# Decode attention over two KV caches: the loads of V issued by GpSimd on a second DMA queue

## The chip, the cores and the metric

The kernel runs on 1 core of one Trainium2 chip. The core has five instruction streams that run side by side and meet only in semaphores: TensorE (PE), VectorE (DVE), ScalarE (ACT), GpSimd (POOL) and SyncE (SP). SP does no arithmetic here; it issues DMAs. The core's 16 DMA engines move the data from HBM (the chip's main memory) to SBUF (the core's working memory) for whichever stream issued the DMA. The metric is the device time of one execution in microseconds, the median of several runs; a smaller number is better.

## The reference

Two independent blocks, A and B, each a one-token decode step of multi-head attention over a cache, with 8 sequences, 32 heads, 4096 cached positions and 128 numbers per head, all in bf16. The outputs are laid side by side.

```
def _A_ref(x, k_cache, v_cache, wq, wo):
    B, Sq, D = x.shape                      # 8, 1, 1024
    H, Dh = 32, 128
    q = transpose((x @ wq).reshape(B, Sq, H, Dh), 0, 2, 1, 3)
    scores = jnp.einsum("bhqd,bhkd->bhqk", q, k_cache) * (Dh ** -0.5)
    p = _softmax(scores, axis=-1)
    o = jnp.einsum("bhqk,bhkd->bhqd", p, v_cache)
    return transpose(o, 0, 2, 1, 3).reshape(B, Sq, H * Dh) @ wo
...
return jnp.concatenate([a, b], axis=-1)     # the same for B
```

Every byte of both K caches and both V caches is read once, and little is done with each: the caches are 4 x 268 MB of the 1107 MB that the kernel moves.

## The kernel before

The work is cut into 64 steps, numbered n: 2 blocks x 4 groups of 8 heads x 8 sequences. One step handles 8 heads of one sequence. Its K is 8 heads x 4096 positions x 128 numbers, 8 MiB, laid out as 128 partitions of 64 KB: each head takes 16 partitions, each partition 256 positions. Its V has the same shape.

In step n the engines do this:

- DVE multiplies K(n) in place by the broadcast query, in four chunks of 64 positions (`multiply`, the costliest DVE line).
- PE adds up each product over the 128 numbers by 16 matmuls against the identity into PSUM (`add_up`), and DVE finishes the sum (`reduce`), chunk by chunk, through two PSUM tiles. DVE then finds the maximum (`softmax`).
- PE multiplies the probabilities of the step before with V(n-1) (`pv`, 64 matmuls).
- ACT takes the eight exponentials (`exps`) into `prob`. There is one `prob`, so `exps(n)` starts only when `pv(n-1)` has read the old one.
- ACT copies the result of `pv` out of PSUM (`copy_o`), PE gathers it (`gather`) and adds up the row sums (`rowsum`), DVE normalises (`heads`, `invert`), and GpSimd copies 128 x 8 numbers to their place (`ona<-on`).

PE runs its stream in order: four `add_up`, then `pv(n-1)`, then in every second step the broadcast of the next two queries (`make_qbc`, from a tile `qg` that GpSimd has filled in `pick_q`), then `gather` and `rowsum`, then the `add_up` of step n+1.

Three buffers hold the caches: `kbuf` has two halves, so K(n) goes to half n % 2, and `vbuf` is one buffer of 8 MiB for V. V(m) can be written only after `pv(m-1)` has read V(m-1). K(n+2) can be written only after the last `add_up(n)` has read the products of K(n). The weights wq, and at the end wo, are loaded through the same buffers.

The order of the work is the order in which the Python code adds operations: a small class, `Program`, keeps a list per engine, derives the waits from the names that each operation reads and writes, drops those that an earlier wait already implies (through `op.clock`), and rolls the steady part into loops. Before the change SP issues all loads of K, V and the weights, in one list: `load_k(n)`, then `load_v(n-1)`, for each n. An issue that has to wait holds the issues behind it. What SP issues goes through one DMA queue, called q1 in the profile; the loads of x and some stores go through ACT's queue, q10.

Of the kernel before, what the change touches and what calls it, by code (L numbers as in the profile page):

```python
# [27 lines left out]
class Program:  # L28
# [33 lines left out]
    def finish(self):  # L62
        for op in self.ops:
            op.deps = [d for d in op.deps if d.dma or d.eng != op.eng or op.eng != "pe"]
            for d in op.deps:
                d.sig = True
        for e in ENGINES:
            ops = self.order[e]
            for a, b, k in self.loops[e]:
                size = (b - a) // k  # L70
                assert size * k == b - a, (e, a, b, k)
                for p in range(a, a + size):
                    if any(ops[p + i * size].sig for i in range(k)):
                        for i in range(k):
                            ops[p + i * size].sig = True
        counts = {}
        for op in self.ops:
            if op.dma:
                counts[op.dma] = counts.get(op.dma, 0) + 16
                op.token = (op.dma, counts[op.dma])  # L80
        for e in ENGINES:
            k = 0
            for op in self.order[e]:
                if op.sig and not op.dma:
                    k += 1
                    op.token = (e, k)
        known = {e: {} for e in ENGINES}
        for op in self.ops:
            mine = known[op.eng]
            waits = {}  # L90
            for d in sorted(op.deps, key=lambda d: -d.token[1]):
                key, val = d.token
                if mine.get(key, 0) >= val:
                    continue
                waits[key] = max(val, waits.get(key, 0))
                for k2, v2 in d.clock.items():
                    if mine.get(k2, 0) < v2:
                        mine[k2] = v2
            op.deps = waits
            op.clock = dict(mine)  # L100
            if op.token:
                op.clock[op.token[0]] = max(op.token[1], op.clock.get(op.token[0], 0))
        return counts
# [40 lines left out]
def _build(nc, caches, out):  # L144
# [23 lines left out]
    with es:  # L168
# [53 lines left out]
        def dma(eng, dst, src, writes, sem, reads=()):  # L222
            return P.add(eng, lambda e: e.dma_start(dst, src), reads=reads, writes=writes, dma=sem)  # L223
# [78 lines left out]
        def source(c, what, b, g):  # L302
            return caches[c][what][b, g * HP:(g + 1) * HP].rearrange("h (p t) d -> (h p) (t d)", t=T)

        def where(n):
            gi, b = divmod(n, B)
            c, g = divmod(gi, NG)
            return c, g, b
# [5 lines left out]
        def load_v(m):  # L314
            c, g, b = where(m)
            buf, name = (vbuf[:], "v") if m < NS - 1 else (kbuf[:, m % 2, :], f"k{m % 2}")
            dma("sp", buf, source(c, 2, b, g), [name], name)
            vplace[m] = (buf, name)

        def load_wo(c):  # L320
# [219 lines left out]
        NS = NC * NG * B  # L540
# [13 lines left out]
        for n in range(NS):  # L554
            m = n - 1
# [9 lines left out]
            if m >= 0:  # L565
                load_v(m)
# [24 lines left out]
            if n == NS - 1:  # L591
                load_v(n)
                project(0, 0)
                write_out(0)
                load_wo(1)
# [128 lines left out]
```

## Time and profile before

| what | value |
|---|---|
| median of 3 runs | 2559.11 us (2558.98 to 2559.45) |
| the profiled execution, its own time | 2558.87 us |
| its span, first to last instruction | 2557.6 us |
| busy: PE, DVE, ACT, POOL | 58%, 53%, 25%, 11% |
| moved by DMA | 1107.49 MB |

The profile shows one execution. A page gives totals, a row of digits for 40 slices of the span, the DMA queues, the chain of work that ended last, and the costliest groups of instructions. A group's row reads: line, engine, operation, output<-inputs, shapes, count | busy us, mean ns of one | idle us of the engine ahead of it and what ended that idle time. The timeline lists instructions by start (us) and duration (us), with the idle time ahead of them in brackets. SPq, ACTq and POOLq are the issuing streams of DMAs.

### The profile page before, as it was taken

The numbers are of one execution on the slowest core, as the hardware profiler recorded it, in microseconds if no ns is written. First come the engines' busy times: TensorE is split into PE (matmuls) and PEld (weight loads), VectorE is DVE, ScalarE is ACT, GpSimd is POOL, SyncE is SP. The second block draws the span as 40 slices with busy tenths as digits, with TensorE's granted clock in tenths as the row PEclk, the third lists the DMA queues.
The fourth block names the chain that finished last, engine by engine and source line by source line (L and its number), as shares of the span: only waits on it lengthen the run. The fifth ranks groups of instructions, "written<-read, shape, count | busy, mean of one in ns | idle before, by whom it ended". The sixth has DMA issues, their size and how long they took to land.

```text
span 2557.6 us, 18705 instructions
## 1 busy us (share of the span) xinstructions
PE 1479.5 (58%) x9322; PEld 286.9 (11%) x5308; DVE 1360.2 (53%) x912; ACT 651.6 (25%) x1129; POOL 291.2 (11%) x112
## 2 busy tenths in 40 slices
PE   3565565565565565565565565565655655655658
PEld 0001101101101101101011011011011011011012
DVE  3455455455465465464565564564564564554551
ACT  0322322312313313313313213223223223223132
POOL 0111011011011011011011011011011110110110
PEclk8787887787887887887877887877877877877879
DMA  9999999999999999999999999999999999999999
GB/s 426 428 439 430 439 430 438 430 439 429 439 430 436 434 433 437 430 438 430 439 430 439 430 439 430 438 432 438 432 436 433 436 432 436 434 433 437 430 439 398
DMA packets 19834, 1107.49 MB, mean 433 GB/s; under 512 B 2240, under 2 KB 2272, under 8 KB 2672
## 3 DMA queue, kind: packets, MB, share of 16 engines
q1 hardware_dynamic: 19744, 1107.31, 99.9%
q8 instruction: 5, 0.08, 0.0%
q10 hardware_dynamic: 80, 0.06, 0.0%
q14 instruction: 5, 0.04, 0.0%
HBM read 1107.33 MB, written 0.03 MB: 433 GB/s over the span
## 4 chain that ended last, share of the span: by engine, by line
DMA 62%; PE 17%; DVE 14%; issue 6%; SPq 1%; another core or an unknown queue 0%; DVEq 0%
DMA kbuf<-in_B_k_cache_dram 31%; DMA kbuf<-in_A_k_cache_dram 30%; PE red L357 12%; DVE kbuf L347 12%; PE oacc L406 4%; DVE osb L369 2%; DMA kbuf<-in_B_wo_dram 1%; SPq L223 0%; PE acc L490 0%; PE late L490 0%; DVE on L433 0%; DVEq L656 0%; PE oacc L255 0%; PE late L255 0%
## 5 line engine op out<-in xcount | busy, mean ns | idle before, releaser
L347 DVE TENSOR_TENSOR kbuf<-kbuf,qbc 128x8192 bf16<-128x8192 bf16 x256 | 1128.3, 4408 | 779.2 <-DMA kbuf<-in_B_k_cache_dram 380.4
L357 PE MATMUL red<-kbuf,ident 128*128 128x512 bf16 x4096 | 1050.0, 418 | 388.4 <-DVE kbuf L347 217.1
L385 ACT ACTIVATE prob<-osb,bias 128x256 bf16<-128x256 f32 x512 | 598.9, 1584 | 904.8 <-PE oacc L406 870.3
L435 POOL COPY ona<-on 128x8 bf16<-128x8 bf16 x64 | 278.7, 4355 | 2211.3 <-DVE on L433 2211.3
L421 PE MATMUL sps<-sel,osb 128*128 128x8 f32 x512 | 116.6, 357 | 650.1 <-ACT osb L413 650.0
L369 DVE TENSOR_REDUCE osb<-red 128x64 f32<-128x512 f32 x256 | 176.2, 688 | 304.9 <-PE red L357 304.9
L385 ACT ACTIVATION_READ_ACCUMULATOR prob<-osb,bias 128x1 f32 x512 | 253.7, 495 | 0.0
L339 ACT ACTIVATE qbc<-bps 128x256 bf16<-128x256 f32 x32 | 12.3, 384 | 899.3 <-PE bps L335 899.3
L406 PE MATMUL oacc<-vbuf,prob 128*32 128x512 bf16 x4032 | 229.1, 380 | 1.2 <-DMA vbuf<-in_B_v_cache_dram 1.2
L421 PEld LDWEIGHTS sps<-sel,osb 128*128 128x128 f32 x512 | 112.4, 323 | 671.7 <-issue 668.2
L357 PEld LDWEIGHTS red<-kbuf,ident 128*128 128x128 bf16 x256 | 25.1, 98 | 1185.7 <-issue 1165.6
L406 PEld LDWEIGHTS oacc<-vbuf,prob 128*32 128x32 bf16 x4032 | 102.0, 97 | 313.3 <-issue 215.6
L413 ACT ACTIVATE osb<-oacc 128x512 f32<-128x512 f32 x64 | 38.3, 598 | 18.1 <-PE oacc L406 11.0
L391 PE MATMUL sps<-rsum,ones 128*128 128x8 f32 x128 | 36.6, 360 | 6.0 <-ACT prob L385 6.0
L391 PEld LDWEIGHTS sps<-rsum,ones 128*128 128x128 f32 x128 | 34.7, 330 | 6.1 <-ACT prob L385 6.1
L374 DVE TENSOR_REDUCE rmax<-osb 128x1 f32<-128x256 f32 x64 | 26.9, 420 | 7.6
L433 DVE TENSOR_TENSOR on<-sps,rl 128x8 bf16<-128x8 f32 x64 | 10.2, 159 | 28.5 <-PE sps L391 28.5
L375 DVE STREAM_TRANSPOSE tmax<-rmax 128x32 f32<-128x32 f32 x64 | 13.5, 211 | 7.7
L376 DVE TENSOR_REDUCE nmax<-tmax 128x2 f32<-128x32 f32 x64 | 12.0, 187 | 7.6
L328 POOL COPY qg<-qT 128x256 bf16<-128x256 bf16 x32 | 12.6, 393 | 27.6 <-DVE qT L300 27.0
L378 DVE SCALAR_TENSOR_TENSOR bias<-nmax,neg 128x8 f32<-128x8 f32 x64 | 10.7, 167 | 7.7
L525 PE MATMUL red<-ident 128*128 128x512 bf16 x58 | 13.5, 380 | 0.0
(64 smaller groups left out, 123.0 us busy)
## 6 DMA issues: line engine op xcount, KB each, us to landing
kbuf<-in_B_wo_dram SPq DMA_DIRECT2D x1, 4096.0 KB, 30.2
kbuf<-in_B_wo_dram SPq DMA_DIRECT2D x1, 2048.0 KB, 34.7
kbuf<-in_B_wo_dram SPq DMA_DIRECT2D x1, 1024.0 KB, 36.7
kbuf<-in_A_k_cache_dram SPq DMA_DIRECT2D x32, 49.0
vbuf<-in_A_v_cache_dram SPq DMA_DIRECT2D x32, 30.1
kbuf<-in_B_k_cache_dram SPq DMA_DIRECT2D x32, 49.1
kbuf<-in_B_wo_dram SPq DMA_DIRECT2D x1, 512.0 KB, 37.4
kbuf<-in_B_wo_dram SPq DMA_DIRECT2D x2, 256.0 KB, 37.7
```

Source lines behind the costliest of these rows:

```text
L347: P.add("dve", lambda e: e.tensor_tensor(kv, kv, qbc[:, n % 2, :].unsqueeze(1).to_broadcast([128, CT, Dh]), ALU.mult), reads=[f"k{n % 2}", ...
L357: first = e.matmul(rv, ident[:], pj[:, :, 0, :], start=True, stop=False).ins
L369: P.add("dve", lambda e: e.tensor_reduce(score[:, ch * CT:(ch + 1) * CT], rv, AX.X, ALU.add), writes=[f"score{ch}"], banks=[f"red{i}"])
L374: P.add("dve", lambda e: e.tensor_reduce(rmax[:], score, AX.X, ALU.max), reads=scores, writes=["rmax"])
L375: P.add("dve", lambda e: e.transpose(tmax[:], rmax[:].to_broadcast([128, 32])), reads=["rmax"], writes=["tmax"])
L385: P.add("act", lambda e, h=h: e.activation(prob[:, :, h], score, ACTF.Exp, bias=bias[:, h:h + 1], scale=scale, accum_out=rsum[:, i, h:h + 1]),
L391: P.add("pe", lambda e: e.matmul(sps[:, i * HP:(i + 1) * HP], ones[:].to_broadcast([128, 128]), rsum[:, i, :], start=True, stop=True), rea ...
L406: last = e.matmul(oacc[32 * q:32 * q + TB * HP, 0:TB * Dh], prob[:, t:t + TB, :].rearrange("p t h -> p (t h)"), buf[:, t * Dh:(t + TB) * D ...
L413: P.add("act", lambda e: e.activation(osb[:], oacc[:], ACTF.Copy), writes=scores, banks=["oacc"])
L421: last = e.matmul(sps[:, o:o + HP], osb[:, t * Dh:(t + 1) * Dh], sel[:, t, :], start=(t == 0), stop=(t == TB - 1))
L435: P.add("pool", lambda e: e.tensor_copy(ona[:, gi, :, b], on[:, i, :]), reads=[f"on{i}"], writes=[f"ona{gi}"])
L525: last = e.matmul(rv, ident[:], ins, start=True, stop=True)
```

## The change

Two lines in two places. `load_v` puts all loads of V but the last two on GpSimd's list instead of SP's, under a semaphore of their own, `vp`. The last two, V(62) and V(63), stay with SP. In `Program.finish`, a DMA issued by GpSimd no longer passes on what its issuer knew when it issued it: whoever waits for such a DMA then makes its other waits itself.

```
@@ Program.finish
             op.deps = waits
-            op.clock = dict(mine)
+            op.clock = {} if op.dma and op.eng == "pool" else dict(mine)
             if op.token:
                 op.clock[op.token[0]] = max(op.token[1], op.clock.get(op.token[0], 0))
@@ _build
         def load_v(m):
             c, g, b = where(m)
             buf, name = (vbuf[:], "v") if m < NS - 1 else (kbuf[:, m % 2, :], f"k{m % 2}")
-            dma("sp", buf, source(c, 2, b, g), [name], name)
+            eng, sem = ("pool", "vp") if m < NS - 2 else ("sp", name)
+            dma(eng, buf, source(c, 2, b, g), [name], sem)
             vplace[m] = (buf, name)
```

On SP, in the first steps, K and V alternate before the change, and each V waits for the `pv` ahead of it (c_pe is PE's semaphore):

```order
L223 DMA vbuf<-in_A_wq_dram 128x32768
L223 DMA kbuf<-in_A_k_cache_dram 128x32768
L223 DMA vbuf<-in_B_wq_dram 128x32768 [waits c_pe,d_v]
L223 DMA kbuf<-in_A_k_cache_dram 128x32768
L223 DMA vbuf<-in_A_v_cache_dram 128x32768 [waits c_pe,d_v]
```

After it, SP's list from the start to the last wo is this:

```order
L223 DMA vbuf<-in_B_wq_dram 128x32768 [waits c_pe,d_v]
L223 DMA kbuf<-in_A_k_cache_dram 128x32768
L223 DMA kbuf<-in_A_k_cache_dram 128x32768 [waits c_pe,c_dve] x30
L223 DMA kbuf<-in_B_k_cache_dram 128x32768 [waits c_pe,c_dve] x32
L223 DMA kbuf<-in_A_wo_dram 128x32768 [waits c_pe,c_dve]
L223 DMA vbuf<-in_B_v_cache_dram 128x32768 [waits c_pe,d_vp]
L223 DMA kbuf<-in_B_v_cache_dram 128x32768 [waits c_pe,c_dve]
```

The loads of V in the middle are gone from it, and each load of K now waits itself, for the `add_up` (PE) and `multiply` (DVE) that read its half of `kbuf`; it no longer stands behind a V that waits for `pv`.

On GpSimd, two steps of the steady part before the change:

```order
L328 COPY qg<-qT 128x256
L435 COPY ona<-on 128x8 [waits c_pool,c_dve] x2
L328 COPY qg<-qT 128x256
L435 COPY ona<-on 128x8 [waits c_pool,c_dve]
L435 COPY ona<-on 128x8 [waits c_dve]
```

and after it:

```order
L223 DMA vbuf<-in_A_v_cache_dram 128x32768 [waits c_pe,d_vp]
L329 COPY qg<-qT 128x256
L436 COPY ona<-on 128x8 [waits c_pool,c_dve]
L223 DMA vbuf<-in_A_v_cache_dram 128x32768 [waits c_pe,d_vp]
L436 COPY ona<-on 128x8 [waits c_pool,c_dve]
```

One load of V stands ahead of the copies of each step, and waits for the `pv` that frees `vbuf`; the copies of that step wait behind it.

More of the change, by code (lines that the diff above doesn't have):

```diff
@@ L99, in finish @@
             op.deps = waits
-            op.clock = dict(mine)
+            op.clock = {} if op.dma and op.eng == "pool" else dict(mine)
             if op.token:
@@ L316, in load_v @@
             buf, name = (vbuf[:], "v") if m < NS - 1 else (kbuf[:, m % 2, :], f"k{m % 2}")
-            dma("sp", buf, source(c, 2, b, g), [name], name)
+            eng, sem = ("pool", "vp") if m < NS - 2 else ("sp", name)
+            dma(eng, buf, source(c, 2, b, g), [name], sem)
             vplace[m] = (buf, name)
```

## The prediction

> **What bounds the kernel now.** I read the totals by queue first, then the busy time of a long stretch in the middle, then the waits of SP and DVE, and last the timeline of one step.
>
> The DMA packets of the whole execution, the queues of SP (q1) and ACT (q10) with their packets, MB and share of the engines' time, and the steady stretch from 110 to 1230 us (busy us of PE, PEld, DVE, ACT and POOL, then granted clock, DMA share, GB/s):
>
> ```profile
> DMA packets 19834, 1107.49 MB, mean 433 GB/s; under 512 B 2240, under 2 KB 2272, under 8 KB 2672
> ...
> q1 hardware_dynamic: 19744, 1107.31, 99.9%
> ...
> q10 hardware_dynamic: 80, 0.06, 0.0%
> ...
> 110.00:1230.00 1120.00, 648.68 (x4040) 124.13 (x2296) 613.10 (x406) 292.90 (x508) 132.73 (x44) 0.80 1.00 434
> ```
>
> SP's one queue keeps all 16 DMA engines busy for 99.9% of the span, at 434 GB/s in the middle, while the busiest engine, PE, works 58% of that stretch. At 434 GB/s the 1107 MB alone take 2552 us of the span of 2557.6, so only 6 us (0.2%) lie outside the transfers. A load of K or V (8.389 MB) takes 19.33 us; a step moves one of each, 38.66 us. A load has 128 rows of 64 KB, so I estimate 8 packets per DMA engine and 19.33 / 8 = 2.42 us for one. The 2240 packets under 512 B are about 16 for each of some 140 DMAs; I take them for the completion marks, one per DMA engine.
>
> Who waits, longest first (engine, line, for whom: us in total, times, longest), SP's queue last:
>
> ```profile
> DVE kbuf L347 <- DMA kbuf<-in_B_k_cache_dram: 380.4, 31, 13.1
> DVE kbuf L347 <- DMA kbuf<-in_A_k_cache_dram: 363.4, 30, 13.1
> ...
> SPq L641 <- PE oacc L406: 2308.8, 62, 39.8
> ```
>
> DVE stands 12 us in each step until its K has landed. SP itself waits nearly all the time for `pv` (line 406), which frees the V buffer; it then issues V(n-1) and K(n+1) at once. It has no issue work that could be saved.
>
> One step in the timeline (start, duration):
>
> ```profile
> 1187.35 3.64 PE L406 MATMUL oacc<-vbuf,prob 128*32 128x512 bf16 x64
> ...
> 1191.08 0.33 SPq L223 DMA_DIRECT2D vbuf<-in_A_v_cache_dram  x1
> ...
> 1191.44 0.43 SPq L223 DMA_DIRECT2D kbuf<-in_A_k_cache_dram  x1
> ...
> 1202.63 4.43 DVE L347 TENSOR_TENSOR kbuf<-kbuf,qbc 128x8192 bf16<-128x8192 bf16 x1 [12.92 <-DMA kbuf<-in_A_k_cache_dram]
> ...
> 1203.49 0.57 PE L391 MATMUL sps<-rsum,ones 128*128 128x8 f32 x2
> ...
> 1207.18 9.62 PE L357 MATMUL red<-kbuf,ident 128*128 128x512 bf16 x32 [3.12 <-DVE on L433]
> ...
> 1227.10 3.64 PE L406 MATMUL oacc<-vbuf,prob 128*32 128x512 bf16 x64
> ...
> 1241.30 4.42 DVE L347 TENSOR_TENSOR kbuf<-kbuf,qbc 128x8192 bf16<-128x8192 bf16 x1 [11.84 <-DMA kbuf<-in_A_k_cache_dram]
> ...
> 1242.77 0.57 PE L391 MATMUL sps<-rsum,ones 128*128 128x8 f32 x2
> ...
> 1245.86 9.06 PE L357 MATMUL red<-kbuf,ident 128*128 128x512 bf16 x32 [2.52 <-DVE on L433]
> ```
>
> and the next `pv`, from the chain of waits:
>
> ```profile
> 1265.30 3.60 PE oacc L406 x64
> ```
>
> From these I take the compute loop, the step if no load were late. From the end of `pv` to the end of `rowsum`: 1190.99 to 1204.06 is 13.07, and 1230.74 to 1243.34 is 12.60; mean 12.85. From the first `add_up` to `pv`: 1207.18 to 1227.10 is 19.92; 1245.86 to 1265.30 is 19.44; mean 19.7. `pv` is 3.64. The sum is 36.2 us, 2.5 us less than the 38.66 us of the transfers. So the kernel is bound by DMA, but compute is only 2.5 us behind, and one V buffer and two K buffers are all the slack there is. PE's other wait, 3.12 and 2.52 us ahead of `add_up`, is those 2.5 us: K landed that much too late.
>
> **The change part by part.** *Issues taken from SP* (62 of 0.33 us): nothing is gained, since SP waits for `pv` and the queue behind it is never empty. *Issues on GpSimd*: its 62 loads wait for `pv`; behind each stands a copy of `ona`, behind every second one of `qg` too.
>
> ```profile
> L435 POOL COPY ona<-on 128x8 bf16<-128x8 bf16 x64 | 278.7, 4355 | 2211.3 <-DVE on L433 2211.3
> ...
> L328 POOL COPY qg<-qT 128x256 bf16<-128x256 bf16 x32 | 12.6, 393 | 27.6 <-DVE qT L300 27.0 <-PE bps L335 0.6
> ...
> vbuf<-in_A_v_cache_dram SPq DMA_DIRECT2D x32, 30.1
> ...
> vbuf<-in_A_wq_dram SPq DMA_DIRECT2D x1, 22.2
> prob<-in_A_x_dram ACTq DMA_DIRECT2D x1, 16.0 KB
> ```
>
> (Group rows of the two copies; then issues with KB where not 8 MiB, and median us to landing.) GpSimd waits 2211 us for DVE; what both copies write is read after the next `pv`, a step later. They cost nothing; were GpSimd to spend 20 us on an issue, `make_qbc` would be late. How long GpSimd takes from its wait to the first packet no row shows: at least SP's 0.33 us, at most its own longest operation, the 4.36 us copy; for an empty queue the wq load on SP shows 22.2 - 19.33 = 2.9 us around a transfer. I take f = 2 us for either queue, the middle of 0.33 to 2.9 rounded up, and keep 2.9 for the range; a longer start of V alone costs little, since K's packets fill it. *The wait for V* on PE (now of `vp`) has the same place; behind it on PE's list stand `gather`, `rowsum` and the next `add_up`. *The `op.clock` line* gives each load of K its own waits for `add_up` and `multiply`, long true or just the condition that matters: nothing.
>
> *The two queues.* This is the part that counts. Now K(n+2) may start when the last `add_up(n)` ends, one `pv` before V(n), and both share the engines. What the engines do with two queues, one place shows, the start, where x goes through ACT's queue beside wq and K(0) on SP's:
>
> ```profile
> 2.13 0.29 ACTq L223 DMA_DIRECT2D prob<-in_B_x_dram  x1
> ...
> 15.75 0.64 PE L271 MATMUL sps<-ident,prob 16*128 16x16 bf16 x8 [15.75 <-DMA prob<-in_B_x_dram]
> ```
>
> Two loads of 16 KB, 0.08 us of transfer, landed 13.6 us after the second issue. Less f that is 11.6, or 4.8 packets of 2.42: a row and a completion mark of each load, each behind about one 64 KB packet of the other queue. So I take turns of one packet. [...]
>
> If V gets a row per turn, two steps go like this, from a moment at which both queues are empty and `add_up` ends. K starts at f = 2, V after `pv` and f, and 16 packets per engine are through at 2 + 38.66 = 40.7. The next `add_up` ends at 36.2, and its K starts to move at 38.2, while V has 2.5 us to go, one packet. Each packet of V and its completion mark now wait for a packet of K: j = 0 to 2 turns of 2.42. Then PE starts `pv`, cold after waiting; the one `pv` in the trace that waited for its V took 5.3:
>
> ```profile
> L406 PE MATMUL oacc<-kbuf,prob 128*32 128x512 bf16 x64 | 5.3, 506 | 2.5 <-DMA kbuf<-in_B_v_cache_dram 2.5
> ```
>
> After it 12.85 + 19.7 = 32.5 us until the next `add_up` ends. In that time V needs f + 19.33 + four turns beside the rest of its K, 31.0, so both queues run empty again. The pair takes 2 + 38.66 + 2.42 j + 0.1 + 5.3 + 32.5 = 78.6 + 2.42 j us, against 77.3 of transfers. j = 0: +1.2 a pair; j = 1: +3.7; j = 2: +6.1; and 0.9 more with f = 2.9. With 31 pairs: +38, +114, +189, and +217 at the upper end. I take j = 1: of the packet left and the mark, one waits on average. The loss appears as DMA idle, some 3 us in every second step.
>
> *Start and end*: wq, K(0), K(1) and the last two V stay in SP's list, and the transfers there are continuous. Nothing.
>
> Sum: 2557.6 + 114 = 2672 for the span; the profiled execution has 1.3 us around its span (2558.87), and the median of the runs is 0.2 us above it. 2673 us, 4.5% slower.
>
> **The rivals.** *Hidden* (not slower): the queues never run empty at the same time, because V's mark waits for no turn and `pv` stays warm at 3.64. The pair is then 76.9, under 77.3: the transfers set the time, 2559. For it speaks that the sum misses the bound by 1 us only at j = 0. It decides where V lands less than 2.5 us after `add_up`. [...] Faster would need engines that move more than 434 GB/s with two queues: each 1% is 62 x 0.39 = 24 us, 2535. No row speaks for it, since the queue is 99.9% full at a constant rate.
>
> *V's whole load in one turn.* V then passes the K in front of it. Two steps run at the compute loop's 36.2, until the backlog has put K(n) behind V(n-1); that step takes f + 19.33 + 2.42 for V and K's last packet, 0.1, and from K's landing to the end of `pv` 28.1 (1202.63 to 1230.74): 52. Three steps are 124.4 against 116, +8.4; 62 / 3 of them +173, 2732. The row of x speaks against it.
>
> *GpSimd's packets are smaller than 64 KB.* A turn then gives V less than K. V's last 2.5 us wait for j = 3 packets of K at 32 KB, 5 at 16 KB, at most the whole load of K (8). The pair is 78.6 + 7.3 = 85.8 (+8.5), 90.7 (+13.3), 97.9 (+20.6): with 31 pairs 2822, 2972, 3197. No row shows a packet of GpSimd's queue, for or against.
>
> **How the numbers follow.** Turns of one row, a loss of j = 0 to 2: 0.48, 2590 to 2780. Whole loads: 0.17, about 2700 to 2750. Small packets: 0.14, of which 32 KB a third. Hidden: 0.17. Faster: 0.03. A V that is slow in itself: 0.01. The range from 2556 to 2830 takes in hidden, single turns, whole loads and 32 KB packets, and leaves out most of the rest; the likeliest case alone has 2590 to 2780. A measurement of this kernel tells 0.2% (5 us) from no change: faster 0.03, same 0.17, slower 0.80.
>
> **What would show it.** A second large queue with about 520 MB, and its packet count: near 62 x 144 for rows of 64 KB, more for smaller ones. V's time to landing near 40 us instead of 30.1. PE or PEld waiting for `vbuf` at line 407, 4 us or more in about half the steps; DVE's 12 us wait for K gone. DMA share and GB/s below 434 in the middle. Step lengths that alternate, about 36 and 45 us; three-step cycles with one of 52 would show whole turns. The forecast is wrong if the mean rate stays at 433 (hidden), if V lands in 21 us and K late (whole turns), or if V takes 45 us or more in every second step (small packets).

## The result and the profile after

| | median of 6 runs | lowest to highest | span of the profiled execution | granted clock |
|---|---|---|---|---|
| before | 2559.05 us | 2558.94 to 2559.45 | 2557.6 us | 0.80 |
| changed | 2708.19 us | 2706.82 to 2709.41 | 2706.8 us | 0.777 |

The ratio is 1.0583, with a 95% interval of 1.0572 to 1.0594. The kernel is 149 us slower; 2673 us (+114) was forecast, with a range of 2556 to 2830.

The DMA packets of the changed kernel (packets, MB, share of the 16 engines' time; q1 is SP's queue, q0 now GpSimd's), and the stretch from 110 to 1230 us (busy us of PE, PEld, DVE, ACT and POOL, granted clock, DMA share, GB/s):

```profile
DMA packets 19834, 1107.49 MB, mean 409 GB/s; under 512 B 2240, under 2 KB 2272, under 8 KB 2672
...
q1 hardware_dynamic: 10816, 587.22, 51.0%
q0 software_dynamic: 8928, 520.10, 44.4%
...
110.00:1230.00 1120.00, 647.79 (x3817) 127.99 (x2179) 582.64 (x386) 272.96 (x473) 138.78 (x67) 0.77 0.96 411
```

GpSimd's queue has 62 x 144 = 8928 packets, so a load of V is still cut into 128 rows of 64 KB and 16 marks. The two queues are busy for 95.4% of 2706.8, 2582 us, against 99.9% of 2557.6, 2555 us. Of the 149 us, 122 are engines with nothing to move and 27 are packets that took longer, most of them K's first ones after an empty stretch (about 3.0 us instead of 2.42).

Who waits for loads now, and the costliest group that this touches:

```profile
PE oacc L407 <- DMA vbuf<-in_A_v_cache_dram: 117.6, 16, 11.6
PE oacc L407 <- DMA vbuf<-in_B_v_cache_dram: 106.0, 15, 7.4
...
DVE kbuf L348 <- DMA kbuf<-in_A_k_cache_dram: 36.3, 3, 20.3
...
L407 PE MATMUL oacc<-vbuf,prob 128*32 128x512 bf16 x4032 | 313.7, 480 | 223.5 <-DMA vbuf<-in_A_v_cache_dram 117.6 <-DMA vbuf<-in_B_v_cache_dram 106.0
```

DVE's 12 us of waiting for K in every step are gone. In their place PE waits for V, 31 times, 7.2 us each. Median times from issue to landing moved the same way, K's from 49.0 to 36.2 us and V's from 30.1 to 39.3. V's median hides two groups: about 39.4 us in the long steps below and 29.2 in the short ones.

Before:

```profile
kbuf<-in_A_k_cache_dram SPq DMA_DIRECT2D x32, 49.0
```

After:

```profile
kbuf<-in_A_k_cache_dram SPq DMA_DIRECT2D x32, 36.2
vbuf<-in_A_v_cache_dram POOLq DMA_DIRECT2D x32, 39.3
```

Two steps in the timeline of the changed kernel (start, duration, idle time ahead):

```profile
1179.74 2.32 PE L358 MATMUL red<-kbuf,ident 128*128 128x512 bf16 x10
1181.99 3.64 PE L407 MATMUL oacc<-vbuf,prob 128*32 128x512 bf16 x64
...
1186.20 0.53 POOL L223 DMA_DIRECT2D vbuf<-in_A_v_cache_dram  x1 [18.49 <-PE bps L336]
...
1215.15 3.61 PE L358 MATMUL red<-kbuf,ident 128*128 128x512 bf16 x16 [1.32 <-DVE kbuf L348]
...
1225.81 6.41 PE L407 MATMUL oacc<-vbuf,prob 128*32 128x512 bf16 x64 [7.04 <-DMA vbuf<-in_A_v_cache_dram]
...
1260.39 3.61 PE L358 MATMUL red<-kbuf,ident 128*128 128x512 bf16 x16 [1.32 <-DVE kbuf L348]
1263.94 3.64 PE L407 MATMUL oacc<-vbuf,prob 128*32 128x512 bf16 x64
```

and the same two steps as windows, from one end of `pv` to the next:

```profile
1185.63:1232.27 46.64, 25.79 (x140) 5.25 (x80) 25.65 (x15) 10.26 (x18) 4.94 (x2) 0.74 1.01 437
1232.27:1267.58 35.31, 21.89 (x140) 4.22 (x80) 16.80 (x13) 9.96 (x17) 5.35 (x3) 0.81 0.88 373
```

A long step of 46.6 us, in which V is late and the engines are full, is followed by a short one of 35.3 us, in which both loads are early and the engines run dry. Over 58 steps in the middle the pair is 81.90 us on average, against 77.31 before. 31 pairs x 4.59 are 142 of the 149 us. Between the first and the last `pv` of the alternating part lie 61 steps, 31 long and 30 short, and they are 148.8 us longer than before; the first `pv` ends 9.2 us later (120.0 against 110.8 us), and what follows the 61 steps takes 8.8 us less.

In the packet records of the long step, K and V alternate packet by packet, 2.42 us each. The marks of V come between 1222.6 and 1222.9 us on 4 of the 16 engines and between 1224.9 and 1225.4 on the other 12, behind a packet of the next K. From about 1261.8 to 1265.0 no packet moves: V has landed, the last `add_up` ends only at 1264.0, and K's first packets begin 1.0 to 1.8 us after SP's issue at 1264.1.

### The profile page after: what moved, and what is told of

Its sections match the earlier page's. It is cut to its first block, busy times and chain, and to the rows that moved or that the text cites. A ratio compares the mean times of both kernels' runs of the same rounds, so it can differ in the third digit from the quotient of the medians.

```text
span 2706.8 us, 18765 instructions
## 1 busy us (share of the span) xinstructions
PE 1564.6 (58%) x9322; PEld 312.4 (12%) x5308; DVE 1365.8 (50%) x912; ACT 652.2 (24%) x1129; POOL 326.9 (12%) x174
## 3 DMA queue, kind: packets, MB, share of 16 engines
q0 software_dynamic: 8928, 520.10, 44.4%
## 4 chain that ended last, share of the span: by engine, by line
DMA 47%; PE 26%; ACT 12%; DVE 11%; issue 3%; another core or an unknown queue 1%; ACTq 0%; DVEq 0%; POOLq 0%; SPq 0%
DMA vbuf<-in_A_v_cache_dram 23%; DMA vbuf<-in_B_v_cache_dram 22%; PE oacc L407 12%; ACT prob L386 11%; PE red L358 11%; DVE kbuf L348 9%; PE sps L422 2%; DVE osb L370 2%; DMA kbuf<-in_A_k_cache_dram 2%; ACT osb L414 1%; PE sps L392 0%; PE acc L491 0%; PE late L491 0%; PE late L255 0%
## 5 line engine op out<-in xcount | busy, mean ns | idle before, releaser
L407 PE MATMUL oacc<-vbuf,prob 128*32 128x512 bf16 x4032 | 313.7, 480 | 223.5 <-DMA vbuf<-in_A_v_cache_dram 117.6
L407 PEld LDWEIGHTS oacc<-vbuf,prob 128*32 128x32 bf16 x4032 | 132.9, 117 | 590.8 <-issue 538.5
L358 PEld LDWEIGHTS red<-kbuf,ident 128*128 128x128 bf16 x256 | 36.7, 143 | 1036.2 <-issue 1013.6
L223 POOL DMA_DIRECT2D vbuf<-in_A_v_cache_dram x32 | 17.0, 532 | 775.2 <-PE oacc L407 440.5
L223 POOL DMA_DIRECT2D vbuf<-in_B_v_cache_dram x30 | 15.8, 528 | 716.3 <-PE oacc L407 439.6
## 6 DMA issues: line engine op xcount, KB each, us to landing
kbuf<-in_A_k_cache_dram SPq DMA_DIRECT2D x32, 36.2
vbuf<-in_A_v_cache_dram POOLq DMA_DIRECT2D x32, 39.3
```

What stands on the lines that cost most here:

```text
L358: first = e.matmul(rv, ident[:], pj[:, :, 0, :], start=True, stop=False).ins
L407: last = e.matmul(oacc[32 * q:32 * q + TB * HP, 0:TB * Dh], prob[:, t:t + TB, :].rearrange("p t h -> p (t h)"), buf[:, t * Dh:(t + TB) * D ...
```

## Experiments

The first theory, that of turns, is the prediction's: two queues with packets of one size share the engines evenly, and with one V buffer both run dry in every second step. Its rival in the first four experiments puts the loss down to GpSimd's queue, whose start is slow. The pair in the table is the mean over 58 steps in the middle, long and short step in brackets where they alternate.

| kernel | median us | ratio to before, 95% interval | pair, us |
|---|---|---|---|
| changed | 2708.2 | 1.0583 [1.0572, 1.0594] | 81.90 (46.5, 35.4) |
| V on ACT's queue | 2707.0 | 1.0584 [1.0566, 1.0601] | 81.92 (45.4, 36.5) |
| V in halves on GpSimd | 2754.9 | 1.0758 [1.0731, 1.0786] | 82.97 (47.2, 35.8) |
| K in halves, V whole on GpSimd | 2565.8 | 1.0028 [1.0016, 1.0039] | 77.19 |
| K in halves, all on SP | 2561.6 | 1.001 [1.0001, 1.002] | |
| four exponentials fewer | 2610.7 | 1.0216 [1.0189, 1.0243] | 78.58 (46.3, 32.3) |
| both in halves | 2658.8 | 1.0397 [1.038, 1.0415] | 80.16 (44.5, 35.7) |
| K in eighths, V whole on GpSimd | 2651.6 | 1.0369 [1.0326, 1.0412] | no pairs |
| four exponentials fewer, all on SP | 2559.0 | 1.0001 [0.9991, 1.001] | |
| PE kept busy ahead of `pv` | 2632.2 | 1.0287 [1.027, 1.0304] | 79.39 (43.2, 36.2) |
| K in quarters, V whole on GpSimd | 2631.6 | 1.0274 [1.0244, 1.0304] | no pairs |
| one exponential fewer | 2660.6 | 1.0402 [1.0385, 1.0419] | 80.49 (45.7, 34.8) |
| one exponential more | 2711.2 | 1.0594 [1.0576, 1.0612] | 81.92 (44.1, 37.8) |

### V on another queue, not GpSimd's

```
-            eng, sem = ("pool", "vp") if m < NS - 2 else ("sp", name)
+            eng, sem = ("act", "vp") if m < NS - 2 else ("sp", name)
...
             if m >= 0:
                 pv(m)
+                if n < NS - 2:
+                    load_v(n)
```

> The loads of V (but the last two) are issued by ACT on its own queue, each right behind the pv that frees the buffer and ahead of the exponentials; K stays on SP. ACT's instructions are written out instead of looped. Theory of turns (two queues take turns packet by packet, and between two steps both run empty): the loss stays whoever issues V; a quicker start of V may save one turn per pair of steps, so 2630 to 2720 us, with long and short steps in turn. Theory of GpSimd (V is late because GpSimd takes some 5 us from pv to the first packet): the loss goes with GpSimd, 2559 to 2575 us.

2707.0 us, the same loss within 1 us. The edit is shown against the changed kernel; the `op.clock` line of the change is not in this kernel either. Its queue (ACT's) and the wait on PE:

```profile
q10 hardware_dynamic: 9008, 520.16, 44.4%
...
PE oacc L407 <- DMA vbuf<-in_A_v_cache_dram: 136.7, 16, 11.4
```

So neither GpSimd nor the `op.clock` line has a part in it: a second queue from another engine loses 148 us.

### The share of the two queues

Rows of 32 KB are half a load each, so the load is two DMAs; who waits for it waits for both. For V:

```
+            w = T * Dh // 2
+            for i, one in enumerate(vn):
+                dma("pool", vbuf[:, i * w:(i + 1) * w], source(c, 2, b, g)[:, i * w:(i + 1) * w], [one], f"vp{i}")
```

> As the changed kernel, but each load of V by GpSimd is two DMAs of half the columns, so that V's rows, and with them its packets, are 32 KB and K's stay 64 KB. Theory of turns: V gets a third of the engines instead of half while K is under way, what is left of V waits for more turns of K, and the time rises to 2770 to 2870 us. Theory of GpSimd: packet sizes do not matter; one more issue of 0.53 us per step, 2708 to 2745 us.

2754.9 us, below the low end of what the theory gave, 47 us above the changed kernel: the direction is right and the size too large. For K, in the changed kernel and in the one before:

```
+            w = T * Dh // 2
+            for i, name in enumerate(kn(n)):
+                dma("sp", kbuf[:, n % 2, i * w:(i + 1) * w], source(c, 1, b, g)[:, i * w:(i + 1) * w], [name], name)
```

> As the changed kernel, but each load of K on SP is two DMAs of half the columns (32 KB rows), V on GpSimd whole (64 KB rows); each multiply waits for both halves, so K is used no earlier. Theory of turns: V gets two thirds of the engines while K is under way, lands in time, and the queues run empty no more: 2557 to 2600 us, DMA at 430 GB/s or more. Theory of GpSimd: nothing that GpSimd does changes, 2700 to 2715 us.

> Control: the kernel before, everything on SP's one queue, with each load of K as two DMAs of half the columns. Both theories: one queue has no turns, so the size of packets alone changes nothing, 2556 to 2566 us.

2565.8 and 2561.6 us. The queues and the waits of the first, K in halves with V on GpSimd:

```profile
q1 hardware_dynamic: 20032, 587.22, 53.1%
q0 software_dynamic: 8928, 520.10, 46.8%
...
DVE kbuf L353 <- DMA kbuf<-in_B_k_cache_dram: 365.0, 31, 17.7
...
PE oacc L412 <- DMA vbuf<-in_A_v_cache_dram: 28.8, 17, 2.5
```

Nothing of GpSimd's part is changed, and 142 of the 149 us are gone. With packets of 32 against 64 KB, V gets about two thirds while both run: in the packet records 2.42 us of V and 1.21 us of K alternate. V lands in time or nearly (PE's 30 waits for it sum to 51 us, against 224 in the changed kernel), DVE waits for K again as in the kernel before, and the queues fill 99.9% of the span. So the loss is a matter of whose load is late. With V in time, `pv` runs right behind `add_up`, the V buffer comes free while K is still moving, and the engines never run dry; with V late, the short step frees a half of `kbuf` and then the V buffer only after both queues have run empty (1261.8 us in the timeline above).

More for V is not better still. K in eighths (`w = T * Dh // 8`) and in quarters, V whole:

> The changed kernel with K in eight DMAs of 8 KB rows on SP and V in one of 64 KB rows on GpSimd. By the theory of turns V gets eight parts in nine, so V passes the K in front of it nearly whole, and K comes late instead: cycles of short steps near 36 us and one of about 50, with DVE waiting for K: 2605 to 2705 us. Rival, that the more V is favoured the better, since only V's lateness costs: 2557 to 2575 us.

> The changed kernel with K in four DMAs of 16 KB rows on SP and V in one of 64 KB rows on GpSimd: between K in halves (2566) and K in eighths (2652). Theory of turns: V gets four parts in five, K begins to be late in some steps: 2570 to 2630 us. Rival, that the loss of K in eighths is the cost of so many small packets and DMAs, not of K coming late: the half of it, 2590 to 2612 us with every step alike and DVE waiting no longer for K than with halves.

2651.6 us is within the first theory's range; 2631.6 is at the upper end of it, just past. Neither has alternating pairs. Most of the steps with K in quarters run 36.5, 35.1, 53.7, 35.1 in a cycle. From the timeline of that kernel, a `pv`, DVE's wait for K, and the next `pv`, 53.6 us later:

```profile
1218.73 3.64 PE L412 MATMUL oacc<-vbuf,prob 128*32 128x512 bf16 x64
...
1247.74 4.42 DVE L353 TENSOR_TENSOR kbuf<-kbuf,qbc 128x8192 bf16<-128x8192 bf16 x1 [26.53 <-DMA kbuf<-in_A_k_cache_dram]
...
1272.30 3.64 PE L412 MATMUL oacc<-vbuf,prob 128*32 128x512 bf16 x64
```

Here V overtakes K, and once in four steps it is K that comes late: DVE waits 26.5 us for it, against 12 in a step of the kernel before. This is the course that the prediction had for whole loads in one turn (a long step of 52), in four steps instead of three. Of the shares tried, two thirds for V is the best, and it only comes back to the time before.

Both in halves:

> The changed kernel with K and V each in two DMAs of 32 KB rows, K on SP and V on GpSimd, so that both queues have packets of one size again. Theory of turns: the share counts and not the size; V and K get half each, both queues still run empty in every second step, the last packet and the mark of V wait for smaller packets: 2640 to 2720 us. Rival, that smaller packets of K cure the loss by themselves: 2560 to 2580 us. A third way, that two DMAs per load of V cost more by their own start: 2740 to 2770 us.

2658.8 us, in the first theory's range: the smaller packet of K alone doesn't cure it, the share does. The reason that I gave for the 49 us gained, a shorter last turn, is the smaller part of what the rows show:

```profile
L418 PE MATMUL oacc<-vbuf,prob 128*32 128x512 bf16 x4032 | 281.2, 440 | 220.6 <-DMA vbuf<-in_A_v_cache_dram 116.7 <-DMA vbuf<-in_B_v_cache_dram 103.8
```

PE waits as long in all as in the changed kernel (220.6 against 223.5 us, though 41 times instead of 31), and 32.5 of the 49 us are a faster `pv` (281.2 against 313.7). Counted from the end of `add_up`, V lands 0.7 us earlier (42.9 against 43.6, means of 28 pairs).

### How near the compute loop is

```
         def exps(n):
...
-            for h in range(HP):
+            for h in range(HP // 2 if n else HP):
```

> The changed kernel with the exponentials of heads 4 to 7 left out of every step after step 0 (their probabilities stay those of step 0, their row sums one); all transfers are as in the changed kernel, and the compute loop is some 4.5 us shorter, about 31.7 us against 38.66 us of transfers. Theory of turns with an empty queue: V has longer to land before the compute loop comes round, so part of the loss goes; a pair of steps falls from 81.9 to at most 79.3, the loss from +149 to about +10 to +80: 2570 to 2640 us. Rival, that the loss lies in the transfers themselves (two queues share the engines badly, whatever compute does): unchanged, 2695 to 2715 us.

> The kernel before with the same exponentials left out (heads 4 to 7 after step 0), everything on SP's queue. Both theories: bound by the transfers as before, 2555 to 2562 us; DVE's wait for K longer by the compute saved.

2610.7 us with V on GpSimd, 2559.0 with all on SP. The second says that the exponentials cost nothing in the kernel before; in the changed kernel half of them are worth 97 us. So the loss isn't one of the transfers by themselves: the second queue has put the compute loop back on the path.

### The cold `pv`

```
+                if m % 2 == 1:
+                    idle(32, warm=True)
                 pv(m)
```

> The changed kernel with 32 matmuls of the identity (0.226 us each at full rate, 7.2 us) on PE ahead of pv in the long step of each pair, in the 7 us in which PE waits for V; nothing reads their result. Theory that the 6.4 us of that pv against 3.64 are PE coming back from idling, and lie on the path: pv falls to about 3.7, a pair from 81.9 to about 79.2, the loss by about 84 us: 2610 to 2640 us. Rival, that pv is slow because V and K still move into the memory that it reads, or that its slowness is covered: 2695 to 2720 us. If the order of long and short steps turns over, the matmuls stand in the short step: 2700 to 2830 us.

2632.2 us, as the first expectation had it. The two steps in its timeline, with the 32 added matmuls (L526) ahead of the late `pv`, and below them its waits, which now lie mostly in the short steps:

```profile
1187.25 7.07 PE L526 MATMUL red<-ident 128*128 128x512 bf16 x32
...
1194.25 3.64 PE L407 MATMUL oacc<-vbuf,prob 128*32 128x512 bf16 x64
...
1230.40 3.64 PE L407 MATMUL oacc<-vbuf,prob 128*32 128x512 bf16 x64 [1.29 <-DMA vbuf<-in_A_v_cache_dram]
```

```profile
PE oacc L407 <- DMA vbuf<-in_A_v_cache_dram: 22.8, 17, 4.4
PE oacc L407 <- DMA vbuf<-in_B_v_cache_dram: 16.9, 16, 1.5
```

The windows of the late `pv` in the changed kernel, and in this one (granted clock third from the right):

```profile
1225.81:1232.22 6.41, 6.41 (x64) 2.65 (x64) 0.00 (x0) 0.00 (x0) 0.00 (x0) 0.56 0.83 358
```

```profile
1194.25:1197.89 3.64, 3.63 (x65) 1.60 (x64) 0.18 (x1) 0.00 (x0) 0.00 (x0) 1.00 0.66 288
```

V still lands when it did (43.5 us after the end of `add_up`, 43.6 in the changed kernel), but PE has not idled, its clock is 1.00 instead of 0.56, and `pv` takes 3.64 us instead of 6.41. Nor is it the traffic into the memory that slows `pv`: in the kernel before it takes the same 3.64 us while the engines move more, 396 against 358 GB/s:

```profile
1187.35:1190.99 3.64, 3.64 (x67) 1.68 (x66) 1.68 (x5) 0.00 (x0) 0.00 (x0) 1.00 0.91 396
```

The faster `pv` is 2.8 us in each of 31 pairs, 86 us by the rows and 76 by the medians: half of the whole loss is TensorE running at a low clock after waiting for V. The 73 us that are left go with V landing late; that both parts go when V lands in time, the kernel with K in halves shows.

### Steps that fall in with the changes of the granted clock

Two quite different kernels, V on GpSimd and V on ACT's queue, had pairs of 81.90 and 81.92 us, and the one with four exponentials fewer 78.58, its usual pair 78.5. In the traces of the kernel before and of the changed one the granted clock is either 1.0 or 0.5, and its 131 and 192 changes all lie multiples of 3.413 us apart; 81.92 is 24 times that, and 78.5 is 23 times. In the long step shown above it goes from 0.5 to 1.0 at 1231.5 us, 5.7 us after the late `pv` has started. Two small changes of the compute loop were to tell whether the steps fall in with these changes:

```
-            for h in range(HP):
+            for h in range(HP - 1 if n else HP):
```

```
-            for h in range(HP):
+            for h in [*range(HP), HP - 1]:
```

> The changed kernel with one exponential of the eight (head 7) left out of every step after step 0, 1.14 us less on the way from the end of pv to the next add_up. The sum of the forecast, in which a pair of steps is the plain sum of its terms: the pair falls by 1.14 us, 35 us in all: 2665 to 2680 us. The rival theory of steps that fall in with the clock gate: the pairs of the changed kernel and of the one with V on ACT's queue are both 81.92 us, 24 times the 3.413 us in which the granted clock changes, because pv, which starts cold after its wait, speeds up at a tick of that grid wherever V's landing falls. Then an earlier start is mostly given back by a longer cold part, up to 7.3 us for a pv that is cold throughout: 2685 to 2709 us.

> The changed kernel with the exponential of head 7 taken twice in every step, 1.14 us more on the same way. Plain sum: the pair grows by 1.14 us, 35 us in all: 2738 to 2748 us. Steps that fall in with the clock gate: the pair stays at 24 ticks, 81.92 us, with a pv of about 5.3 instead of 6.4 us: 2703 to 2712 us.

One exponential more left the time nearly where it was, 2711.2 us, and the pairs at 24 ticks: 28 of 29 lie within 0.05 of it. That refutes the plain sum as I had written it. But `pv` didn't give way as I had written either; it took 6.3 us still. From the timeline and the landings of this kernel:

```profile
1223.23 6.27 PE L407 MATMUL oacc<-vbuf,prob 128*32 128x512 bf16 x64 [3.56 <-DMA vbuf<-in_A_v_cache_dram]
```

```profile
vbuf<-in_A_v_cache_dram POOLq DMA_DIRECT2D x32, 37.0
```

V lands about one turn of 2.42 us earlier than in the changed kernel (37.0 us after its issue instead of 39.3). One exponential less gave 48 us back, more than the plain sum's 35 and below both ranges: 2660.6 us, its pairs between 79.6 and 82.4 us, without a fixed length. So neither theory had the smaller change right; the second had the time of the larger one, though not its `pv`.

What takes up the difference can be read from the traces. The terms of a pair are those of the forecast; the figures are means of 28 pairs in the middle, in us. The pair is the sum of V's landing, the late `pv` and the last column, and 0.1 us from landing to `pv`.

| kernel | `add_up` ended, until V landed | PE's wait | late `pv` | until the next `add_up` ended | pair |
|---|---|---|---|---|---|
| changed | 43.6 | 7.1 | 6.4 | 31.8 | 81.9 |
| V on ACT's queue | 43.7 | 8.3 | 5.1 | 33.0 | 81.9 |
| one exponential more | 41.3 | 3.5 | 6.3 | 34.2 | 81.9 |
| one exponential fewer | 43.9 | 8.6 | 5.7 | 30.8 | 80.5 |
| four exponentials fewer | 46.1 | 12.8 | 5.2 | 27.2 | 78.6 |
| PE kept busy ahead of `pv` | 43.5 | 7.2 | 3.6 | 31.9 | 79.4 |

Two things stand out. V's landing moves by whole turns: 41.3, 43.6 and 46.1 us. In the packet records of the steps looked at, with one exponential more V's marks come ahead of the next K on all 16 engines; in the changed kernel the marks of 12 engines wait for one packet of that K; with four exponentials fewer V's last packet waits for one packet and the marks for a second. The sooner the `add_up` in between ends and lets the next K in (37.9, 36.7 and 33.5 us after the one before), the more turns V loses. With one exponential more the last column grew by 2.4 us (1.5 ahead of the first `add_up`, 0.9 in the four `add_up`, at a granted clock of 0.86 instead of 0.90), and the turn that V no longer lost paid for it.

And the late `pv` doesn't grow with the wait: it takes 6.3 us after 3.5 us of waiting, 5.1 after 8.3 and 5.2 after 12.8. Why it has this length in one kernel and that in another, and what holds three different sums at 24 ticks, stays open; the lengths show only that they are held (in the changed kernel V's landing varies by 0.12 us and the pair by 0.05, as standard deviations).

No kernel beat the one before. There was little room: its transfers alone take 2552 of its 2557.6 us.

## Why the prediction was right

**The bound.** That the kernel before is bound by one full queue held: with half of the exponentials left out it took the same time, 2559.0 us. The compute loop was sized well: the short step, in which no load is late, takes 35.4 us, 0.8 less than the 36.2 that were forecast.

**Issues, copies, the wait's place.** All taken as nothing. The waits and the steps show none of them: GpSimd spends 0.53 us on an issue, and with ACT issuing V instead the time is the same.

**Turns of one packet, an even share.** Right. The packet count is 62 x 144, the records alternate K and V, and the time follows the share when the size of either side's packets is changed: 2754.9 with V at half the size, 2565.8 with K at half. The records of both queues show one row of 64 KB at a time, 2.42 us each. The three-step cycle of whole loads did not come in the changed kernel.

**Alternating steps and dry queues.** Right: about 45 and 36 us were named, 46.5 and 35.4 came.

**The size of the loss.** Forecast +114, measured +149. The time lies in the range of the likeliest case alone, 2590 to 2780; the whole range began at 2556 and would have held no change as well. The pair, term by term, from the end of `add_up` (1179.74 + 2.32 = 1182.06):

| term | forecast | measured |
|---|---|---|
| `add_up` ended, until V landed: 2 + 38.66 + 2.42 | 43.1 | 43.7 (to 1225.8) |
| late `pv` | 5.3 | 6.4 |
| from its end to the next end of `add_up` | 32.5 | 31.7 (1232.2 to about 1264) |
| pair | 81.0 | 81.9 |

One turn lost (j = 1) was the right choice among 0 to 2 for this kernel, and it is V's mark that loses it on 12 of 16 engines. But it was a guess, an average of the three: kernels one exponential more and four fewer lose none and two. The term that was mis-sized is `pv` after a wait. I took 5.3 us from the only such row there was, after 2.5 us of waiting, though the forecast's own sum has PE wait 7 us; here `pv` took 6.4 at a mean granted clock of 0.56. The length of the wait doesn't give it, as the table of pairs shows, so the 5.3 was as good a guess as any from one row. Over 31 pairs its 1.1 us are 34 us. The landing (+0.6) and the chain behind `pv` (-0.8) take 6 of them back, and the 7 us by which the loss exceeds 31 mean pairs make up the 35. The forecast also held j fixed; an edit of 1 us in the compute loop can gain or lose a whole turn.

**The rivals.** *Hidden*: refuted, V lands 7 us after `add_up` in every second step, not less than 2.5. Its other case, Faster, too: 411 GB/s in the middle. Issuing V from a second engine saved nothing here and cost 149 us, since it also changed the order in which the loads are served. *Whole loads*: refuted for 64 against 64 KB; the course it named, V ahead of K and DVE then waiting for K (26.5 us in the timeline above), came where V's packets are four or eight times K's, but it cost 72 to 93 us, not 173, since the long step comes about every fourth time. *Smaller packets on GpSimd*: refuted by the count. Its price was too high as well: V at 32 KB was to cost 2822, and with V cut that way by hand it is 2755.

## What to carry to other kernels

In these runs a single queue served the loads in the order written; two queues served them by turns of one packet (2.42 us for 64 KB), and the time followed the size of the packets (2565.8 us with K's at half of V's, 2754.9 with V's at half of K's). Before a stream is moved to a queue of its own, ask which load is waited for at the end of the chain: give that one the larger packets (here twice as large; four and eight times made the other load late), or leave it in the one queue ahead of the others. A wait moved to TensorE can also slow the work behind it: after 3.5 to 12.8 us of waiting `pv` took 5.1 to 6.4 us instead of 3.64, so count that separately.

## What the hardware showed that I had not expected

- Half of the loss, 76 us, was TensorE's clock after a 7 us wait (0.56 granted). A longer wait did not make it worse: after 12.8 us `pv` took 5.2 us instead of 6.4.
- In four kernels the repeating pair of steps was as long as a multiple of the 3.413 us in which the granted clock changes in the traces: 24 ticks in three kernels, about 23 in one. One exponential more in each step cost 3 us in all, one less gave 48.
- The marks that complete one load came up to 2.8 us apart: on 4 of the 16 engines at once, on the other 12 behind a packet of the other queue (2.42 us). V counted as landed at 1225.7 us, after the last mark at 1225.4.
